# Turning the experts' rows on VectorE instead of TensorE, in an attention plus mixture-of-experts kernel

## The chip, the cores and the metric

The kernel runs on one core of a Trainium2 chip. A core has a matrix engine (TensorE, in the profile PE; PEld is its loading of the stationary operand), a vector engine (VectorE, DVE), an activation engine (ScalarE, ACT), a general one (GpSimd, POOL) and a sync engine (SP) that here only issues DMAs. Each engine works through its own queue in program order, and engines wait for one another by semaphores. The metric is the device time of one execution in microseconds (us), the median of several runs. Lower is better. The profile is of one execution, and its span is somewhat shorter than the timed runs.

## The reference, cut to what matters

Attention with a causal mask and a decay, then one expert of eight for each token. All data is float32.

```python
B, H, S, D = 8, 8, 576, 64             # attention
scores = q @ k.T / sqrt(D)
cum = cumsum(maximum(s, 0))
scores += minimum(-(cum[:, None] - cum[None, :]), 0)      # causal: later keys masked
x = softmax(scores) @ v                # heads side by side: (8, 576, 512)

E, F = 8, 1024                         # experts, rows of 512
logits = x @ w_gate
local_gate = sigmoid(x @ w_local)
for each batch b, position s:
    fresh_e = argmax(logits[b, s])
    e = fresh_e if s == 0 or local_gate[b, s] < 0.5 else prev_e
    prev_e = e
    h = maximum(x[b, s] @ w1[e], 0)    # 512 -> 1024, relu
    out[b, s] = softmax(logits[b, s])[e] * (h @ w2[e])    # 1024 -> 512, scaled by the gate
```

## The kernel before

The first part is attention, 32 pairs of heads, one step for each and one more. Beside it the tokens are sorted by expert: their rows are scattered to a buffer in DRAM (`rows_d`), each expert's rows one after another, with the token's number and its gate at the end of each row. The second part, `experts`, works through 26 units: two early ones of experts 0 and 1, and 24 that tables name at run time: "double" (256 rows of one expert), "single" (128 rows) and "mixed" (two halves of 64 rows of two experts). A block of 128 rows comes in with tokens on the partitions. The first layer needs it turned, features on the partitions, as `xT`. In the kernel before, TensorE turns a block by four transposes (128x128 each) into one PSUM bank, and VectorE copies the bank to `xT`. Then come the first layer into banks `hp` with a relu to `hT`, the second layer into a bank `yp`, the scaling of `yp` by the gate to `y`, and the scattering of `y`'s rows to the output.

The turning:

```python
    def __init__(self, nc, fx, gp, ident):
        self.nc, self.fx, self.gp, self.ident = nc, fx, gp, ident
        self.xT, self.at, self.gate = {}, {}, {}

    def product(self, i, k, n, x, ps):

        ps = self.ps = ps.rearrange("p (c n) -> p c n", c=DK)
        for c in range(DK):
            self.nc.tensor.transpose(ps[:, c, :], x[:, 2 * c * HW + X0 : 2 * c * HW + X0 + P], self.ident)
        if k == 0:
            self.xT[i] = self.fx.tile([P, DK * 2 * P], F32, name="xT")[:, : DK * n * P].rearrange(
                "p (c n) -> p c n", c=DK)

    def copies(self, i, k, x):

        nc = self.nc
        nc.vector.tensor_copy(self.xT[i][:, :, k * P : k * P + P], self.ps)
        both = self.gp.tile([P, 2], I32, name="at_gate")
        self.at[i, k], self.gate[i, k] = both[:, 0:1], both[:, 1:2].bitcast(F32)
        nc.vector.tensor_copy(self.at[i, k], x[:, XI : XI + 1])
        nc.vector.tensor_copy(self.gate[i, k], x[:, XI + 1 :])


```

In `experts` (the code for mixed units and the loads is cut):

```python
    ps_x = pool("ps_x", 1, space=PSUM)
    ps_h = pool("ps_h", 2, space=PSUM)
    ps_y = pool("ps_y", 2, space=PSUM)
    ps_r = pool("ps_r", 3, space=PSUM)
    # ... cut
    def turn_x(i, k):
        if i >= NU or k >= nbs[i]:
            return
        ps = ps_x.tile([P, DK * P], F32, name="xp")
        x = xg.pop((i, k))
        turned.product(i, k, nbs[i], x, ps)
        turned.copies(i, k, x)


    def layer1(i, first, last):
        # ... cut
        per = 512 // n
        for g in range(first, last, per):
            ps = ps_h.tile([P, 512], F32, name="hp")
            for j in range(per):
                f = (g + j) * P
                y = ps[:, j * n : j * n + n]
                if len(w) == 1:
                    for c in range(DK):
                        mm(y, lhsT=w[0][:, c, f : f + P], rhs=xT[i][:, c, :], start=(c == 0), stop=(c == DK - 1))
                # ... cut: mixed units, hooks
            to = hT[i][:, g : g + per]
            if g // per % 2:
                nc.vector.tensor_scalar_max(to, ps, 0.0)
            else:
                nc.scalar.activation(to, ps, Act.Relu)

    def layer2(i, k, then):
        ps = ps_y.tile([P, D], F32, name="yp")
        w = [ws[s][:, DK * F :].rearrange("p (c d) -> p c d", c=FK) for s in of[i]]
        m = P // len(w)
        for c in range(FK):
            for n, wn in enumerate(w):
                a = k * P + n * m
                mm(ps[n * m : n * m + m, :], lhsT=hT[i][:, c, a : a + m], rhs=wn[:, c, :],
                   start=(c == 0), stop=(c == FK - 1))
            if c in then:
                turn_x(*then[c])
            tick()
        y = gp.tile([P, D], F32, name="y", bufs=3)
        nc.vector.tensor_scalar_mul(y, ps, gate[i, k])
        nc.gpsimd.indirect_dma_start(
            out=next(outs)[:, :], out_offset=bass.IndirectOffsetOnAxis(ap=at[i, k][:, 0:1], axis=0),
            in_=y[:, :], element_offset=0, bounds_check=N - 1, oob_is_err=False, in_offset=None)

    def second(i):

        for k in range(nbs[i]):
            layer2(i, k, {3: (i + 2, k)} if nbs[i] == 2 else {1: (i + 2, 0), 5: (i + 2, 1)})
```

The order of the units; `load` requests weights, `fetch` requests rows, both ahead of their use:

```python
    layer1(0, 0, 4)
    turn_x(1, 0)
    layer1(0, 4, FK - 2 if nbs[0] == 2 else FK)
    turn_x(1, 1)
    if nbs[0] == 2:
        layer1(0, FK - 2, FK)
    if ready:

        layer1(1, 0, FK)
        load(0)
        fetch(2)
        fetch(3)
        for k in range(2):
            layer2(0, k, {})
        load(1)
        for k in range(2):
            layer2(1, k, {1: (2 + k, 0), 5: (2 + k, 1)})
        load(2)
        layer1(2, 0, 4)
        fetch(4)
        layer1(2, 4, FK)
    else:
        fetch(2)
    for i in range(2 if ready else 0, NU):
        load(i)
        layer1(i + 1, 0, 4)
        fetch(i + 3)
        layer1(i + 1, 4, FK)
        second(i)
```

The first unit's rows come in near the end of attention, and are turned in its steps 30 and 31:

```python
        at(27, 1, fetch_early)
        # ... cut
        for i in range(2):
            at(30 + i, 1, lambda bank, i=i: turned.product(0, i, 2, ready["x"][0, i], bank(1)[0]))
            at(30 + i, 2, lambda bank, i=i: turned.copies(0, i, ready["x"].pop((0, i))))
```

The last group of tokens (batches 6 and 7) is still sorted while the first expert units run: its instructions are hung between their matmuls (`tick`).

## Time and profile before

| | |
|---|---|
| time, median of 3 runs | 829.06 us (828.01 to 829.65) |
| span of the profiled execution | 815.2 us |
| attention, start to the first matmul of the experts | 0 to 248.1 us |
| last matmul ends, about | 808.3 us |
| mean granted clock of TensorE | 0.997 |

How to read the page: the first part gives each engine's busy time, share of the span and number of instructions. The second cuts the span in 40 slices and gives each engine's busy share in tenths. Groups of instructions are told by their line in the kernel, the engine, the operation, the tiles written and read, their shapes and number; behind the bar stand the busy time in us, the mean duration of one in ns, and how long the engine had idled before them and for whom. The groups that the change touches, beside the matmuls:

```profile
L1210 ACT ACTIVATE hT<-hp 128x512 f32<-128x512 f32 x38 | 22.7, 597 | 506.8 <-PE hp L1195 422.9
...
L1208 DVE TENSOR_SCALAR hT<-hp 128x512 f32<-128x512 f32 x38 | 26.2, 690 | 223.7 <-PE hp L1195 187.7
...
L1225 DVE TENSOR_SCALAR y<-yp,at_gate 128x512 f32<-128x512 f32 x38 | 28.5, 750 | 135.6 <-PE yp L1219 135.6
...
L1086 DVE COPY xT<-xp 128x512 f32<-128x512 f32 x36 | 24.9, 691 | 81.8 <-PE xp L1078 81.7
```

These are 38 relus on ScalarE and 38 on VectorE, 38 scalings of the output, and 36 copies of turned blocks (two more blocks, of the first unit, are turned in attention into a tile `bank`). A timeline lists instructions in order of time: start in us, duration of the run in us, engine, line, operation, tiles, shape, number, and in brackets the idle time before and its releaser. TensorE's matmuls in float32 show as two records each, its transposes as one.

### The profile page before, as it was taken

How to read it: one execution, taken by the hardware profiler on the slowest of the kernel's cores; microseconds unless marked ns; L12 is line 12 of the kernel's file. 1: busy time of each engine (PE TensorE's matmuls, PEld its weight loads, DVE VectorE, ACT ScalarE, POOL GpSimd, SP SyncE). 2: the span in 40 equal slices, each digit the busy share in tenths (PEclk: the TensorE clock that was granted, in tenths of full speed). 3: DMA queues.
4: the chain of work that ended last, by engine and by line, in shares of the span. 5: the costliest groups of instructions: out<-in, count | busy, mean ns of one | idle time of the engine just before them, and what ended most of it. 6: DMA issues, size and time to landing. Idle time of an engine off the chain costs nothing.

```text
span 815.2 us, 19716 instructions
## 1 busy us (share of the span) xinstructions
PE 798.7 (98%) x8118; PEld 595.9 (73%) x8118; DVE 213.9 (26%) x700; ACT 188.5 (23%) x535; POOL 176.4 (22%) x329
## 2 busy tenths in 40 slices
PE   9999999999999999999999899998999999999996
PEld 8989888888888748666776666775667766676762
DVE  2234434545535831111111111111111111111111
ACT  5767677576671000000000000000000000000000
POOL 4422344365350421001200011001111011011001
PEclk9999999999999999999999999999999999999999
DMA  9486589788735799678993779946599766994001
GB/s 323 146 293 199 165 266 328 267 275 254 230 135 208 213 402 393 252 249 292 358 388 142 248 254 362 389 174 248 161 358 391 273 200 203 358 411 151 21 15 42
DMA packets 64149, 204.57 MB, mean 251 GB/s; under 512 B 8269, under 2 KB 8301, under 8 KB 64048
## 3 DMA queue, kind: packets, MB, share of 16 engines
q1 hardware_dynamic: 55008, 172.41, 60.6%
q0 software_dynamic: 8896, 30.47, 9.9%
q8 instruction: 66, 1.08, 0.5%
q10 hardware_dynamic: 144, 0.33, 0.1%
q14 instruction: 35, 0.29, 0.1%
HBM read 179.93 MB, written 23.76 MB: 250 GB/s over the span
## 4 chain that ended last, share of the span: by engine, by line
PE 98%; issue 1%; POOL 0%; DVE 0%; POOLq 0%
PE yp L1219 32%; PE hp L1195 29%; PE o L407 13%; PE ps L329 11%; PE hp L1202 4%; PE o L369 2%; PE xp L1078 2%; PE o L285 1%; PE o L350 1%; PE bank L946 1%; PE bank L971 0%; PE bank L944 0%; PE bank L969 0%; PE bank L992 0%; PE bank L1078 0%
## 5 line engine op out<-in xcount | busy, mean ns | idle before, releaser
L1219 PE MATMUL yp<-w,hT 128*128 128x512 f32 (+1 forms) x528 | 221.1, 594 | 0.0
L1195 PE MATMUL hp<-xT,w 128*128 128x256 f32 (+1 forms) x1088 | 192.1, 337 | 0.0
L1195 PEld LDWEIGHTS hp<-xT,w 128*128 128x128 f32 x1088 | 172.1, 191 | 23.8 <-issue 7.8
L338 ACT ACTIVATE sc<-ps,bias 128x256 f32<-128x256 f32 (+3 forms) x448 | 156.5, 482 | 57.0 <-PE ps L329 55.0
L1219 PEld LDWEIGHTS yp<-w,hT 128*128 128x128 f32 (+1 forms) x528 | 88.0, 180 | 100.5 <-issue 99.5
L1210 ACT ACTIVATE hT<-hp 128x512 f32<-128x512 f32 x38 | 22.7, 597 | 506.8 <-PE hp L1195 422.9
L1226 POOL DMA_INDIRECT out_dram<-y,at_gate x38 | 38.5, 1012 | 461.7 <-DVE y L1225 446.8
L407 PEld LDWEIGHTS o<-v,sc 128*64 128x64 f32 x3072 | 108.8, 136 | 7.9 <-issue 5.2
L407 PE MATMUL o<-v,sc 128*64 128x74 f32 x3072 | 113.6, 229 | 0.1
L344 POOL TENSOR_SCALAR_AFFINE_SELECT sc<-sc 128x256 f32<-128x256 f32 x160 | 66.5, 420 | 122.0 <-issue 64.3
L329 PE MATMUL ps<-q,k 64*128 64x320 f32 (+2 forms) x768 | 92.2, 385 | 0.3 <-issue 0.3
L1208 DVE TENSOR_SCALAR hT<-hp 128x512 f32<-128x512 f32 x38 | 26.2, 690 | 223.7 <-PE hp L1195 187.7
L329 PEld LDWEIGHTS ps<-q,k 64*128 64x128 f32 x768 | 68.9, 186 | 15.1 <-ACT r_v L956 0.6
L1219 PE MATMUL yp<-x,hT 128*128 128x512 f32 (+1 forms) x144 | 65.6, 601 | 0.0
L1225 DVE TENSOR_SCALAR y<-yp,at_gate 128x512 f32<-128x512 f32 x38 | 28.5, 750 | 135.6 <-PE yp L1219 135.6
L1195 PEld LDWEIGHTS hp<-xT,x 128*128 128x128 f32 x320 | 46.1, 191 | 5.8 <-issue 2.6
L1195 PE MATMUL hp<-xT,x 128*128 128x128 f32 (+1 forms) x320 | 50.1, 317 | 0.0
L1086 DVE COPY xT<-xp 128x512 f32<-128x512 f32 x36 | 24.9, 691 | 81.8 <-PE xp L1078 81.7
L1037 POOL DMA_INDIRECT x_rows<-x,r_slot_i x40 | 38.7, 968 | 10.0 <-issue 5.9
L1219 PEld LDWEIGHTS yp<-x,hT 128*128 128x128 f32 (+1 forms) x144 | 25.0, 181 | 21.8 <-issue 21.4
L1202 PE MATMUL hp<-xT,w 128*64 128x64 f32 x768 | 32.5, 227 | 6.4 <-issue 6.4
L1202 PEld LDWEIGHTS hp<-xT,w 128*64 128x64 f32 x768 | 31.4, 141 | 9.9 <-issue 9.9
(164 smaller groups left out, 412.9 us busy)
## 6 DMA issues: line engine op xcount, KB each, us to landing
w<-in_w_dram SPq DMA_DIRECT2D x184, 512.0 KB, 10.1
x<-in_w_dram SPq DMA_DIRECT2D x56, 512.0 KB, 10.1
v<-in_vx_dram SPq DMA_DIRECT2D x32, 370.0 KB, 5.3
vt<-in_vz_dram SPq DMA_DIRECT2D x32, 320.0 KB, 4.1
k<-in_kz_dram SPq DMA_DIRECT2D x31, 320.0 KB, 5.3
q<-in_q_dram SPq DMA_DIRECT2D x32, 288.0 KB, 5.9
xg<-x_rows POOLq DMA_DIRECT2D x30, 293.0 KB, 8.3
x_rows<-r_empty SPq DMA_DIRECT2D x6, 293.0 KB, 5.0
```

The source lines that it names most:

```text
L329: mm(ps[:, h, at : at + z - a], lhsT=kb[d, c * P : c * P + P], rhs=qb[d, a:z], start=True, stop=True)
L338: nc.scalar.activation(scs[n, u][:, h, at : at + z - a], raw[u][:, h, at : at + z - a], Act.Exp, bias=bias[:, i : i + 1], scale=scale)
L344: nc.gpsimd.affine_select(out=x, in_=x, compare_op=Alu.is_ge, fill=0.0, base=0, pattern=[[0, 2], [1, P]], channel_multiplier=-1)
L407: mm(y, lhsT=w, rhs=x, start=start, stop=stop)
L1037: self.s.nc.gpsimd.indirect_dma_start(out=next(self.s.views)[:, :], out_offset=bass.IndirectOffsetOnAxis(ap=self.slot[:z, m : m + 1], axis=0),
L1086: nc.vector.tensor_copy(self.xT[i][:, :, k * P : k * P + P], self.ps)
L1195: mm(y, lhsT=w[0][:, c, f : f + P], rhs=xT[i][:, c, :], start=(c == 0), stop=(c == DK - 1))
L1202: mm(y[d, m], lhsT=w[h ^ swap][:, c, f + h * HALF : f + h * HALF + HALF], rhs=xT[i][:, c, m], start=(c == 0), stop=(c == DK - 1))
L1208: nc.vector.tensor_scalar_max(to, ps, 0.0)
L1219: mm(ps[n * m : n * m + m, :], lhsT=hT[i][:, c, a : a + m], rhs=wn[:, c, :], start=(c == 0), stop=(c == FK - 1))
L1225: nc.vector.tensor_scalar_mul(y, ps, gate[i, k])
L1226: nc.gpsimd.indirect_dma_start(out=next(outs)[:, :], out_offset=bass.IndirectOffsetOnAxis(ap=at[i, k][:, 0:1], axis=0), in_=y[:, :], eleme ...
```

## The change

Three things. VectorE turns the rows of all units but the second: one of its instructions turns 32 rows by 4 x 32 features, four squares of 32x32, and writes them to the 32 partitions of `xT` where they belong; 16 of them make a block, and no PSUM bank or copy is needed. They are issued a first layer ahead, before the first layer of the unit in between, instead of within the second layer of the unit two before. The first unit's rows are turned so in the last steps of attention, a quarter block or some at a time; the second unit's are still turned by TensorE. To make room on VectorE, the relus of the first layer and the scaling of the second layer's output all go to ScalarE. The PSUM bank that took the turned rows becomes a third one for the first layer.

```diff
--- before.py
+++ after.py
@@ -147,9 +147,10 @@
 
         fx = main.enter_context(tc.tile_pool(name="fx", bufs=2))
         turned = ready["turned"] = Turned(nc, fx, main.enter_context(tc.tile_pool(name="first", bufs=2)), ident)
-        for i in range(2):
-            at(30 + i, 1, lambda bank, i=i: turned.product(0, i, 2, ready["x"][0, i], bank(1)[0]))
-            at(30 + i, 2, lambda bank, i=i: turned.copies(0, i, ready["x"].pop((0, i))))
+        for j in range(8):
+            at((29, 29, 30, 30, 30, 31, 31, 31)[j], 2,
+               lambda bank, j=j: turned.squares(0, j // 4, 2, ready["x"][0, j // 4], (j % 4,)))
+        at(31, 2, lambda bank: [turned.extras(0, k, ready["x"].pop((0, k))) for k in range(2)])
         last = sort.group((6, 7), xs)
 
         attention(tc, q, kz, vz, vx, s, w_gate, w_local, ident, lg, recs, const, new_x, plan)
@@ -1071,19 +1072,33 @@
         self.nc, self.fx, self.gp, self.ident = nc, fx, gp, ident
         self.xT, self.at, self.gate = {}, {}, {}
 
+    def new(self, i, k, n):
+        if k == 0 and i not in self.xT:
+            self.xT[i] = self.fx.tile([P, DK * 2 * P], F32, name="xT")[:, : DK * n * P].rearrange(
+                "p (c n) -> p c n", c=DK)
+
+    def squares(self, i, k, n, x, quarters=range(4)):
+
+
+        self.new(i, k, n)
+        rows = x[:, :XI].rearrange("p (c w) -> p c w", w=2 * HW)
+        m = P // 4
+        for a in quarters:
+            for d in range(0, P, m):
+                self.nc.vector.transpose(self.xT[i][d : d + m, :, k * P + a * m : k * P + a * m + m],
+                                         rows[a * m : a * m + m, :, X0 + d : X0 + d + m])
+
     def product(self, i, k, n, x, ps):
 
-        ps = self.ps = ps.rearrange("p (c n) -> p c n", c=DK)
+        self.new(i, k, n)
+        ps = ps.rearrange("p (c n) -> p c n", c=DK)
         for c in range(DK):
             self.nc.tensor.transpose(ps[:, c, :], x[:, 2 * c * HW + X0 : 2 * c * HW + X0 + P], self.ident)
-        if k == 0:
-            self.xT[i] = self.fx.tile([P, DK * 2 * P], F32, name="xT")[:, : DK * n * P].rearrange(
-                "p (c n) -> p c n", c=DK)
-
-    def copies(self, i, k, x):
+        self.nc.vector.tensor_copy(self.xT[i][:, :, k * P : k * P + P], ps)
+
+    def extras(self, i, k, x):
 
         nc = self.nc
-        nc.vector.tensor_copy(self.xT[i][:, :, k * P : k * P + P], self.ps)
         both = self.gp.tile([P, 2], I32, name="at_gate")
         self.at[i, k], self.gate[i, k] = both[:, 0:1], both[:, 1:2].bitcast(F32)
         nc.vector.tensor_copy(self.at[i, k], x[:, XI : XI + 1])
@@ -1111,8 +1126,7 @@
     wp = pool("wp", 1)
     gp = pool("gp", 8)
     fp = pool("fp", 2)
-    ps_x = pool("ps_x", 1, space=PSUM)
-    ps_h = pool("ps_h", 2, space=PSUM)
+    ps_h = pool("ps_h", 3, space=PSUM)
     ps_y = pool("ps_y", 2, space=PSUM)
     ps_r = pool("ps_r", 3, space=PSUM)
     gx = gx or pool("gx", 5)
@@ -1168,13 +1182,15 @@
                     row = number(sort.rowi[kinds[kind]], j, ET.Pool, E * R)
                 nc.gpsimd.dma_start(x, rows_d[bass.ds(row + k * P, P), :])
 
-    def turn_x(i, k):
+    def turn_x(i, k, by_products=False):
         if i >= NU or k >= nbs[i]:
             return
-        ps = ps_x.tile([P, DK * P], F32, name="xp")
         x = xg.pop((i, k))
-        turned.product(i, k, nbs[i], x, ps)
-        turned.copies(i, k, x)
+        if by_products:
+            turned.product(i, k, nbs[i], x, bank(1)[0])
+        else:
+            turned.squares(i, k, nbs[i], x)
+        turned.extras(i, k, x)
 
     def layer1(i, first, last):
 
@@ -1203,13 +1219,10 @@
                                    rhs=xT[i][:, c, m], start=(c == 0), stop=(c == DK - 1))
                 for _ in range(nbs[i]):
                     tick()
-            to = hT[i][:, g : g + per]
-            if g // per % 2:
-                nc.vector.tensor_scalar_max(to, ps, 0.0)
-            else:
-                nc.scalar.activation(to, ps, Act.Relu)
-
-    def layer2(i, k, then):
+
+            nc.scalar.activation(hT[i][:, g : g + per], ps, Act.Relu)
+
+    def layer2(i, k):
         ps = ps_y.tile([P, D], F32, name="yp")
         w = [ws[s][:, DK * F :].rearrange("p (c d) -> p c d", c=FK) for s in of[i]]
         m = P // len(w)
@@ -1218,19 +1231,16 @@
                 a = k * P + n * m
                 mm(ps[n * m : n * m + m, :], lhsT=hT[i][:, c, a : a + m], rhs=wn[:, c, :],
                    start=(c == 0), stop=(c == FK - 1))
-            if c in then:
-                turn_x(*then[c])
             tick()
         y = gp.tile([P, D], F32, name="y", bufs=3)
-        nc.vector.tensor_scalar_mul(y, ps, gate[i, k])
+        nc.scalar.activation(y, ps, Act.Copy, scale=gate[i, k])
         nc.gpsimd.indirect_dma_start(
             out=next(outs)[:, :], out_offset=bass.IndirectOffsetOnAxis(ap=at[i, k][:, 0:1], axis=0),
             in_=y[:, :], element_offset=0, bounds_check=N - 1, oob_is_err=False, in_offset=None)
 
     def second(i):
-
         for k in range(nbs[i]):
-            layer2(i, k, {3: (i + 2, k)} if nbs[i] == 2 else {1: (i + 2, 0), 5: (i + 2, 1)})
+            layer2(i, k)
 
     if ready:
         ws[1] = room[1]
@@ -1240,34 +1250,40 @@
         fetch(0)
         fetch(1)
     if not ready:
-        for k in range(nbs[0]):
-            turn_x(0, k)
+        for i in range(2):
+            for k in range(2):
+                turn_x(i, k)
     tick(0)
     layer1(0, 0, 4)
-    turn_x(1, 0)
-    layer1(0, 4, FK - 2 if nbs[0] == 2 else FK)
-    turn_x(1, 1)
-    if nbs[0] == 2:
+    if ready:
+        turn_x(1, 0, True)
+        layer1(0, 4, FK - 2)
+        turn_x(1, 1, True)
         layer1(0, FK - 2, FK)
-    if ready:
 
         layer1(1, 0, FK)
         load(0)
         fetch(2)
         fetch(3)
         for k in range(2):
-            layer2(0, k, {})
+            layer2(0, k)
         load(1)
         for k in range(2):
-            layer2(1, k, {1: (2 + k, 0), 5: (2 + k, 1)})
+            turn_x(2, k)
+        second(1)
         load(2)
+        for k in range(2):
+            turn_x(3, k)
         layer1(2, 0, 4)
         fetch(4)
         layer1(2, 4, FK)
     else:
+        layer1(0, 4, FK)
         fetch(2)
     for i in range(2 if ready else 0, NU):
         load(i)
+        for k in range(2):
+            turn_x(i + 2, k)
         layer1(i + 1, 0, 4)
         fetch(i + 3)
         layer1(i + 1, 4, FK)
```

## The prediction

> **What bounds the kernel now.** I read the busy shares first, then the chain of waits, then the groups of instructions, and last the timelines around the instructions that the change touches.
>
> ```profile
> PE 798.7 (98%) x8118; PEld 595.9 (73%) x8118; DVE 213.9 (26%) x700; ACT 188.5 (23%) x535; POOL 176.4 (22%) x329
> ...
> PE 98%; issue 1%; POOL 0%; DVE 0%; POOLq 0%
> PE yp L1219 32%; PE hp L1195 29%; PE o L407 13%; PE ps L329 11%; PE hp L1202 4%; PE o L369 2%; PE xp L1078 2%; PE o L285 1%; PE o L350 1%; PE bank L946 1%; PE bank L971 0%; PE bank L944 0%; PE bank L969 0%; PE bank L992 0%; PE bank L1078 0%
> ```
>
> The matrix engine (PE) is busy for 98% of the 815.2 us span and is 98% of the chain that ended last. So the end moves by what leaves PE's own queue, or by new holes in it, and hardly by anything else. The turning of the experts' rows (xp, line 1078) is 2% of that chain: this is the whole prize. VectorE (DVE) and ScalarE (ACT) are about a quarter busy over all. By stages DVE is busy 38.7 us of the 92 us from 248 to 340 and 70.6 us of the 475 us after that; ACT 5.9 and 17.9 us.
>
> What a turned block of 128 rows costs PE is not its duration but the time to the next start. A typical one, in the timeline of PE:
>
> ```profile
> 401.43 0.60 PE L1078 MATMUL xp<-ident,xg 128*128 128x128 f32 x4
> 401.86 1.88 PE L1219 MATMUL yp<-w,hT 128*128 128x512 f32 x4
> ```
>
> From 401.43 to 401.86 is 0.43 us for four transposes, though each lasts 273 ns: they overlap. I went through all of PE's timeline from 250 to 790 us this way. Nearly every block costs 0.43 to 0.44 us, the four turned inside mixed units 0.58 or 0.59. In attention the two blocks of unit 0 take 0.59 us (236.55 to 237.14) and 0.73 us (243.95 to 244.68).
>
> On DVE, the end of attention:
>
> ```profile
> 244.28 0.19 DVE L374 COPY v<-o 128x45 f32<-128x45 f32 x1
> 244.39 0.19 DVE L375 COPY v<-o 128x45 f32<-128x45 f32 x1
> 244.64 0.69 DVE L1086 COPY xT<-bank 128x512 f32<-128x512 f32 x1
> 245.25 0.15 DVE L1089 CAST at_gate<-xg 128x1 int32<-128x1 f32 x1
> 245.31 0.15 DVE L1090 COPY at_gate<-xg 128x1 f32<-128x1 f32 x1
> 247.01 0.18 DVE L409 RECIPROCAL recs<-o 128x4 f32<-128x4 f32 x1 [1.56 <-PE o L407]
> ```
>
> The reader is to see the hole of 1.56 us before 247.01, the only room in this last step. The two small copies are 0.06 us apart though each lasts 0.15: DVE's instructions can overlap. PE starts the experts' first layer at 248.14.
>
> [...] 36 copies of 0.69 us follow the 144 transposes. [...] the trace has one table load (1.28 us) though exp and relu both run, [...] so a scaled copy should add none.
>
> **The change, part by part.** There are 38 blocks of 128 rows: 2 of unit 0 (in attention), 2 of unit 1, 34 of the others. Unit 1 stays on PE.
>
> (1) Taken from PE in the experts: 34 blocks, 30 at 0.437 us and 4 at 0.58: 13.1 + 2.3 = 15.4 us. (2) Taken from PE in attention: 0.59 + 0.73 = 1.3 us. Both lie on the chain, and together they are 16.7 us.
>
> (3) Added to DVE: 36 blocks of 16 transposes, each 32 partitions by 128 elements. Estimate of one from this trace: a copy of one element takes 144 ns, and copies of 45 and 512 elements take 195 and 691, a slope of 1.06 ns an element; so 144 + 127 x 1.06 = 279 ns. Held, 16 of them are 4.5 us a block and 161 us in all; overlapped as the small copies are, about 0.2 us apart, 3.2 us a block. Taken from DVE: 36 copies of 0.69 (24.9), 38 relus (26.2), 38 scalings (28.5), in all 79.6 us. DVE then stands near 295 us, a third of the span.
>
> (4) Added to ACT: 38 relus of 0.597 (22.7 us) and 38 scalings, which should be near that. A PSUM bank of the first layer takes PE 3.44 us to fill and ACT 0.6 to empty, and there are now three banks for it in place of two, so PE doesn't wait there.
>
> (5) Moved: a unit's rows are now turned during the first layer of the unit ahead of it, and needed after that unit's whole second layer. A double unit is 28 us of PE and 9 us of DVE, a single one 14 and 4.5. Its rows were requested one unit earlier still and land in about 8.3 us. The slot of xT that is overwritten belongs to a first layer that is already over. I see no wait for PE in the steady part. The tightest place is unit 2: its rows are requested at 287.1 to 288.3 and land near 295, DVE would turn them by about 304 to 305, and PE reaches them at 308.8 less what was saved until then (some 2 us): a slack of 2 us.
>
> (6) The end of attention. With the 0.59 us of the step before gone, DVE's last copy ends near 244.0. Then come 12 transposes: 3.4 us held, 2.4 overlapped, and four small copies. So xT is whole at about 247.4, while PE, 1.3 us early, asks for it at 246.8: a wait of 0.6 us, or none if they overlap. The last batch's reciprocals slip behind them too, but its routing on PE comes 5.2 us later and DVE has caught up by then.
>
> (7) The tail: the last scaling takes 0.75 us on DVE and some 0.6 on ACT: 0.15 gained.
>
> Sum: 15.4 + 1.3 - 0.6 + 0.15 = 16.2 us. 829.06 - 16.2 = 812.8; I round to 813.0, since small holes are likelier than small gifts.
>
> **The rivals.** (a) DVE becomes a wait: if one transpose took 0.5 us and not 0.28, a block would take 8 us, the wait at the end of attention 3 us, and unit 2 another 5; the gain would shrink to some 8 us, near 821. For it: no such instruction runs before, so its length is an estimate. Against it: in the steady part even this fits into the 14 us of a single unit.
>
> (b) Instruction supply. PE has unexplained holes in the mixed units' first layers:
>
> ```profile
> 356.37 3.01 PE L1202 MATMUL hp<-xT,w 128*64 128x64 f32 x94 [0.46 <-issue]
> ...
> 567.07 2.09 PE L1202 MATMUL hp<-xT,w 128*64 128x64 f32 x36 [3.38 <-issue]
> ```
>
> They add up to 6.4 us in four places, named issue and no engine, in stretches with many short instructions and busy DMA queues. A shift of 2% in time can make them larger or smaller; I allow 2 us either way, and the change touches neither cause.
>
> (c) The transfer of weights takes the place of PE: if the weights came no faster than they do now, an earlier PE would wait for them. Against it: the DMA share is 67% after 340 us and no wait of PE names a DMA; the sync queue itself waits 233 us for PE to release weight buffers. From 281 to 330 us the queues are full (over 400 GB/s), and there some of the gain might be lost for a while. That would make the gain some 14 us, or 815.
>
> (d) More than is counted: should the waits of (b) vanish, up to 6 us more, 807.
>
> **Range and chances.** Two per cent is 16.6 us, or 812.5, so the estimate sits almost on the line between two of the verdicts. The sum of what leaves PE is firm to half a microsecond; the wait at the end of attention is 0 to 1 us; the holes move it by 2 us. That gives 810.0 to 817.0 for 8 in 10, with more room above for (a) and (c). Faster by over 2%: 0.43. Within 2%: 0.54. Slower by over 2%: 0.03, since nothing that is added lies on PE.
>
> **What would show it.** PE's transposes should fall from 152 to 8, and PE's busy time by 16 to 17 us. The transposes on DVE should last near 0.28 us and follow each other at that distance. The first matmul of the experts should show a wait of about half a microsecond on DVE, and unit 2's first none. DVE should be near 295 us busy, ACT near 235. The prediction is wrong if PE's busy time falls as said and the span doesn't, which would be a new wait in front of a first layer, or if the transposes last far from 0.28 us, or if the holes of the mixed units change by more than 2 us.

## The result, and the profile after

The changed kernel takes 809.48 us (median; 807.45 to 810.63) against 828.53 us (827.79 to 829.65) for the kernel before in the same comparison. The ratio is 0.9766, with a 95% interval of 0.9742 to 0.9791: 19.05 us are gained. I had predicted 16.2 us and 813.0. The measured time lies half a microsecond under the range of 810 to 817.

The experiments ran on four chips: e1 to e4, e5 to e8, e9 to e11 and e12 to e15. The kernel before takes 827 to 829 us on three of them and 816 us on that of e9 to e11; its first profile, with a span of 815.2 us, looks like this last one. So I took a second profile of the kernel before, e1, whose span of 824.2 us is the one to hold against the 805.8 us of after.

The page after, first the busy shares, then three groups of instructions (busy time, mean ns of one, idle before):

```profile
PE 786.0 (98%) x7974; PEld 583.2 (72%) x7974; DVE 310.6 (39%) x1164; ACT 236.6 (29%) x611; POOL 174.5 (22%) x329
...
L1088 DVE STREAM_TRANSPOSE xT<-xg 32x128 f32<-32x128 f32 x576 | 174.1, 302 | 272.3 <-DMA xg<-x_rows 167.6
...
L1223 ACT ACTIVATE hT<-hp 128x512 f32<-128x512 f32 x76 | 45.1, 597 | 226.1 <-PE hp L1211 183.1
...
L1236 ACT ACTIVATE y<-yp,at_gate 128x512 f32<-128x512 f32 x38 | 26.1, 687 | 239.3 <-PE yp L1232 233.2
```

PE has 144 matmuls fewer, and is still 98% busy: it remains the bound. Its busy time is 18.2 us less than in e1 (804.2), where 16 to 17 were predicted. DVE has more work by nearly a half, and waits for rows 167.6 us, so it is far ahead of PE in the experts. All relus and scalings now stand in ACT's list.

The same place as in the prediction, a single unit's second layer. In the timeline of PE of e1, the kernel before:

```profile
405.19 1.88 PE L1219 MATMUL yp<-w,hT 128*128 128x512 f32 x4
406.91 0.60 PE L1078 MATMUL xp<-ident,xg 128*128 128x128 f32 x4
407.34 3.60 PE L1219 MATMUL yp<-w,hT 128*128 128x512 f32 x8
410.78 0.60 PE L1078 MATMUL xp<-ident,xg 128*128 128x128 f32 x4
411.22 1.88 PE L1219 MATMUL yp<-w,hT 128*128 128x512 f32 x4
412.94 1.24 PE L1195 MATMUL hp<-xT,w 128*128 128x256 f32 x5
```

In that of after:

```profile
403.37 7.03 PE L1232 MATMUL yp<-w,hT 128*128 128x512 f32 x16
410.24 2.11 PE L1211 MATMUL hp<-xT,w 128*128 128x256 f32 x9
```

From the first start to the next layer's: 7.75 us before, 6.87 after. Two blocks are gone, 0.44 us each, as predicted.

DVE at the end of attention, in the timeline of after, and PE at the experts' first matmul, in its own:

```profile
251.46 3.79 DVE L1088 STREAM_TRANSPOSE xT<-xg 32x128 f32<-32x128 f32 x12
```

```profile
255.39 5.42 PE L1211 MATMUL hp<-xT,w 128*128 128x256 f32 x24 [0.34 <-DVE xT L1088]
```

Twelve transposes in 3.79 us: one starts 0.32 us after the other and lasts 0.30. They don't overlap. PE waits 0.34 us for the last of them.

**Where the time went, by stages.** Each stage runs from its first matmul on PE to the next stage's first; the numbers (us) are worked out from PE's timelines, and the differences from the times before rounding. "Mixed" are the first layers of the four mixed units, "first two" those of units 0 and 1.

```
                              e1 (before)   after   difference
attention, to experts' start     254.6      255.4      +0.75
first two first layers            32.7       34.5      +1.7
mixed first layers, four          39.6       36.0      -3.55
all other first layers           210.6      210.6       0
all second layers                279.9      262.5     -17.3
after the last matmul              6.8        6.8       0
span                             824.2      805.8     -18.4
```

Of the 17.3 us of the second layers, 30 blocks at 0.44 are 13.2. The four blocks in mixed units are 0.73 each (the second layer goes from 7.75 to 7.02 us), 2.9 together. That is 16.1. The remaining 1.2 us are holes that sit in second layers. In e1, for example, the stage after the third mixed first layer takes 14.92 us, and the same stage after the other three 14.28.

So there are three places to explain: the mixed first layers gain 3.55 us that I had put down as zero, the first two first layers lose 1.7, and attention gains nothing. PE's waits show the first. Columns: total us, how often, the longest. The kernel before (e1):

```profile
PE hp L1202 <- issue: 6.1, 3, 3.0
...
PE hp L1195 <- DVE hT L1208: 1.0, 1, 1.0
```

After:

```profile
PE hp L1218 <- issue: 3.2, 4, 1.3
...
PE hp L1211 <- issue: 2.5, 3, 1.7
...
PE hp L1211 <- DVE xT L1088: 0.3, 1, 0.3
```

Line 1202 of before is line 1218 of after, the mixed units' matmuls. Their holes named "issue" fall from 6.1 to 3.2 us, and nothing of the change is meant for them. Lines 1195 and 1211 are the other units' matmuls. Before, PE waits 1.0 us there for a relu of DVE; after, it has three holes of 2.5 us in sum, which its timeline has between 286.3 and 289.6, in unit 1's first layer.

### The profile page after: what moved, and what is told of

Its sections match the earlier page's. It is cut to its first block, busy times and chain, and to the rows that moved or that the text cites. A ratio compares the mean times of both kernels' runs of the same rounds, so it can differ in the third digit from the quotient of the medians.

```text
span 805.8 us, 19973 instructions
## 1 busy us (share of the span) xinstructions
PE 786.0 (98%) x7974; PEld 583.2 (72%) x7974; DVE 310.6 (39%) x1164; ACT 236.6 (29%) x611; POOL 174.5 (22%) x329
## 4 chain that ended last, share of the span: by engine, by line
issue 58%; POOL 4%; POOLq 1%; DMA 0%; SPq 0%
POOL out_dram L1237 2%; POOL xg L1183 2%; POOLq L1158 1%; DMA x_rows<-r_empty 0%; SPq L808 0%; POOLq L1183 0%; POOLq L1237 0%; POOL xg L1179 0%; POOLq L1179 0%; POOLq L166 0%; SPq L804 0%
## 5 line engine op out<-in xcount | busy, mean ns | idle before, releaser
L1088 DVE STREAM_TRANSPOSE xT<-xg 32x128 f32<-32x128 f32 x576 | 174.1, 302 | 272.3 <-DMA xg<-x_rows 167.6
L1232 PE MATMUL yp<-w,hT 128*128 128x512 f32 (+1 forms) x528 | 216.4, 593 | 0.0
L1232 PEld LDWEIGHTS yp<-w,hT 128*128 128x128 f32 (+1 forms) x528 | 90.1, 180 | 113.1 <-issue 111.4
L408 PE MATMUL o<-v,sc 128*64 128x74 f32 x3072 | 118.3, 229 | 4.0 <-issue 3.1
L408 PEld LDWEIGHTS o<-v,sc 128*64 128x64 f32 x3072 | 111.2, 136 | 13.4 <-issue 9.8
L1223 ACT ACTIVATE hT<-hp 128x512 f32<-128x512 f32 x76 | 45.1, 597 | 226.1 <-PE hp L1211 183.1
L1236 ACT ACTIVATE y<-yp,at_gate 128x512 f32<-128x512 f32 x38 | 26.1, 687 | 239.3 <-PE yp L1232 233.2
L1232 PE MATMUL yp<-x,hT 128*128 128x512 f32 (+1 forms) x144 | 63.3, 594 | 0.0
L410 DVE RECIPROCAL recs<-o 128x4 f32<-128x4 f32 x64 | 12.1, 189 | 91.7 <-PE o L408 84.1
```

Of the source, the lines that this page charges most:

```text
L408: mm(y, lhsT=w, rhs=x, start=start, stop=stop)
L1088: self.nc.vector.transpose(self.xT[i][d : d + m, :, k * P + a * m : k * P + a * m + m], rows[a * m : a * m + m, :, X0 + d : X0 + d + m])
L1223: nc.scalar.activation(hT[i][:, g : g + per], ps, Act.Relu)
L1236: nc.scalar.activation(y, ps, Act.Copy, scale=gate[i, k])
```

## The experiments

The theories at the start. A: the gain is PE's own turning, 16 us, and a shift of the mixed units' holes, some 3 us; the work moved to ACT is worth nothing. B: freeing DVE from relus and scalings, with the third PSUM bank, is what brings the rest. C: the three microseconds above 16 are the chip's. For the last runs A was made sharper: the holes come from the supply of instructions, in pages of fixed size, so the number of instructions ahead of a mixed unit sets where in it the hole lies and how long it is.

**e1: the kernel before, unchanged.** No edit.

> The kernel before, unchanged, for a second profile. Theory A (the first profile's span of 815.2 us is an unusual execution, the usual one has more holes on PE during attention): the span lies near 826 us, the extra 10 us or so lie before the experts' first matmul, which then comes near 258 us and not 248, and the experts' part stays near 567 us. Rival B (the usual execution is slower in the experts' part, where the change then gains more than I counted): attention near 248 us, experts near 578.

Measured: ratio 1.0007 [0.9991, 1.0023], 827.58 us. The two profiles of before differ by 9 us in span, and their stages say where: attention 248.1 against 254.6, the first two first layers 31.4 against 32.7, the mixed ones 38.8 against 39.6. The second layers agree to half a microsecond (279.4 and 279.9). Of the 9 us, 6.5 lie in attention, so A of the expectation holds in the main. C falls for the second layers: the 17 us that the change takes out of them are there with either profile of before, and e5, on another chip than e1 to e4, has the 262.5 us of after again. Attention's time varies by 6.5 us between these two profiles of one kernel, and so a saving of one microsecond there can't be seen between two profiles.

**e2: the turning left out of the kernel before.** Of units 2 to 25 the rows are copied to `xT` unturned. It leaves the transposition out, so the output isn't the reference's; copies, relus and scaling stay as they were.

```diff
-        turned.product(i, k, nbs[i], x, ps)
+        if i < 2:
+            turned.product(i, k, nbs[i], x, ps)
+            turned.copies(i, k, x)
+            return
+        turned.ps = x[:, :XI].rearrange("p (c w) -> p c w", w=2 * HW)[:, :, X0 : X0 + P]
...
```

> The kernel before, but the 34 turned blocks of the later units leave out PE's transposes: VectorE copies the rows to xT unturned, so the output is not the reference's. Theory A (PE's transposes cost what the timeline showed, 0.43 to 0.58 us a block, and nothing more): 15.4 us less than before, ratio 0.981. Rival B (a turned block costs more in the usual execution, by what it does to PE's instruction supply or to waits): 18 us or more less, ratio 0.978 or below.

Measured: 0.9716 [0.9672, 0.9760], 804.73 us: 22.7 us less than the kernel before, so A of the expectation (15.4) falls and B (18 or more) holds. The second layers take 262.8 us, as after the change (262.5): the 17 us come from leaving out PE's transposes and from nothing else of the change. The mixed first layers take 34.5 us in place of 39.6, and the holes named "issue" shrink though nothing in those stages was edited. In the waits of PE of e2 line 1209 is the mixed units' matmul:

```profile
PE hp L1209 <- issue: 1.8, 4, 0.7
```

**e3: the first unit turned by PE.** The changed kernel, with unit 0 turned in attention as before.

```diff
-        for j in range(8):
-            at((29, 29, 30, 30, 30, 31, 31, 31)[j], 2,
-               lambda bank, j=j: turned.squares(0, j // 4, 2, ready["x"][0, j // 4], (j % 4,)))
...
+        for i in range(2):
+            at(30 + i, 1, lambda bank, i=i: turned.product(0, i, 2, ready["x"][0, i], bank(1)[0]))
...
```

> The changed kernel, but the first unit's rows are turned by TensorE in attention as before. Theory A (turning them on VectorE is worth 0.7 us, 1.3 saved and 0.6 lost in the wait at the first matmul): 0.7 us slower than the changed kernel, ratio to before 0.977 to 0.978. Rival B (the extra gain comes from attention): 3 us or more slower than the changed kernel, ratio 0.980 or above.

Measured: 0.9751 [0.9709, 0.9792], 807.14 us, not to be told from after. Attention takes 255.5 us (255.4 after). This part of the change, for which I had counted 0.7 us net, is worth nothing that these runs can see; a difference so small would be lost in what attention varies by. Beside it the mixed first layers take 33.7 us here, 2.3 less than after, and the second layers 264.1, 1.6 more, though only eight transposes in attention were put back.

**e4: only the work moved to ACT.** The kernel before, with all relus and the scaling of `y` on ACT.

```diff
-            to = hT[i][:, g : g + per]
-            if g // per % 2:
-                nc.vector.tensor_scalar_max(to, ps, 0.0)
-            else:
-                nc.scalar.activation(to, ps, Act.Relu)
+            nc.scalar.activation(hT[i][:, g : g + per], ps, Act.Relu)
...
-        nc.vector.tensor_scalar_mul(y, ps, gate[i, k])
+        nc.scalar.activation(y, ps, Act.Copy, scale=gate[i, k])
```

> The kernel before with only the relus and the scaling of the output moved to ScalarE; rows are turned by TensorE as before. Theory A (PE never waited for either): 0.15 us gained at the tail, ratio 0.999 to 1.001. Rival B (relus on VectorE held PE up somewhere in the usual execution): 2 to 3 us gained, ratio 0.997.

Measured: 1.0083 [1.0054, 1.0111], 833.98 us: this part alone makes the kernel before slower, and B falls as far as it does without a third bank (e8 has one). The waits of PE say by what:

```profile
PE hp L1195 <- ACT hT L1206: 6.6, 1, 6.6
PE hp L1202 <- issue: 5.2, 3, 3.3
```

One wait of 6.6 us for a relu, in the first layer of unit 1: the first two first layers take 41.1 us. ACT stands still there: it waits for nothing in the program that the trace shows. The same is seen after the change, in ACT's timeline:

```profile
276.64 0.60 ACT L1223 ACTIVATE hT<-hp 128x512 f32<-128x512 f32 x1 [2.86 <-PE hp L1211]
289.55 1.57 ACT L1223 ACTIVATE hT<-hp 128x512 f32<-128x512 f32 x3 [12.31 <-remote]
```

Three relus in a row at 289.55: the banks had long been full. ACT did nothing for 12.31 us, and the releaser that the trace gives, "remote", is no engine of this program. With three banks PE goes on filling banks for most of that time, with holes of 2.5 us in sum; with two it waits 6.6 us here. The holes of PE after the change that were left open above belong to this stand: the last of them ends at 289.56, when ACT starts again, and in e3, e5 and e12 too PE and ACT start again within 0.03 us of each other, though the trace calls PE's holes "issue"; in e9 and e10, where ACT doesn't stand, that layer has no holes. The kernel before has a wait of ACT of this length too (12.51 us in e1, where the trace names PE), but there DVE does every second relu, and PE loses 1.0 us by it.

**e5: the changed kernel again**, on the chip of the next three. No edit.

> The changed kernel, unchanged, as the measure of the other three on the same chip: ratio to before 0.974 to 0.979. In its profile the four first layers of the mixed units take 33.5 to 36.5 us together (39.6 in the kernel before), and the first two units' first layers about 34.5 (32.7 before).

Measured: 0.9779 [0.9754, 0.9804], 811.93 us. Attention takes 262.0 us here, the first two first layers 34.6 (ACT's stand is there again), the second layers 262.5, the mixed first layers 35.8.

**e6: two banks in place of three** in the changed kernel.

```diff
-    ps_h = pool("ps_h", 3, space=PSUM)
+    ps_h = pool("ps_h", 2, space=PSUM)
```

> The changed kernel with two PSUM banks for the first layer in place of three. Theory A (moving every relu to ScalarE costs some 6 to 7 us while ScalarE stands still in the second unit's first layer, and the third bank is what lets PE run past most of it): 4 to 6 us slower than the changed kernel, ratio to before 0.982 to 0.984, and the first two units' first layers take 39 to 41 us. Rival B (the third bank does nothing, PE is paced by its own instructions): no difference, 0.976.

Measured: 0.9818 [0.9790, 0.9846], 815.33 us; beside e5 3.4 us more, with intervals that just overlap. In the waits of PE:

```profile
PE hp L1211 <- ACT hT L1223: 6.7, 1, 6.7
```

The first two first layers take 40.9 us, 6.3 more than in e5, and the rest of the experts is as there to half a microsecond. The total differs by less than the expected 4 to 6 us. Attention, which the edit doesn't touch, takes 257.3 us in this profile and 262.0 in that of e5. So the third bank is needed only where ACT stands, in one stage, and there it hides some 6 us of it. In the rest of the experts two banks did as well.

**e7: every second relu of units 0 and 1 on DVE**, the rest as changed.

```diff
-            nc.scalar.activation(hT[i][:, g : g + per], ps, Act.Relu)
+            if ready and i < 2 and g // per % 2:
+                nc.vector.tensor_scalar_max(hT[i][:, g : g + per], ps, 0.0)
+            else:
+                nc.scalar.activation(hT[i][:, g : g + per], ps, Act.Relu)
```

> The changed kernel, but in the first two units every second relu is done by VectorE as before. Theory A (the 1.7 us that the first two units' first layers lost are ScalarE's stand): 1 to 2 us faster than the changed kernel, the first two first layers back at 32.5 to 33 us. Rival B (VectorE is late there too, with the routing of the last tokens): no gain, 34 us or more.

Measured: 0.9748 [0.9700, 0.9796], 809.23 us, 2.7 us under e5 with overlapping intervals. The first two first layers fall from 34.6 (e5) to 32.7 us, and the second layers of units 0 and 1 rise from 27.5 to 28.6: more than half is given back. Half of the relus avoid the ACT that stands; that the other half still wait for it is the likely reason, not a shown one.

**e8: squares only.** The changed kernel with relus alternating and the scaling on DVE, as before the change.

```diff
-            nc.scalar.activation(hT[i][:, g : g + per], ps, Act.Relu)
+            to = hT[i][:, g : g + per]
+            if g // per % 2:
+                nc.vector.tensor_scalar_max(to, ps, 0.0)
+            else:
+                nc.scalar.activation(to, ps, Act.Relu)
...
-        nc.scalar.activation(y, ps, Act.Copy, scale=gate[i, k])
+        nc.vector.tensor_scalar_mul(y, ps, gate[i, k])
```

> The changed kernel with relus and scaling where they were: every second relu and all scalings on VectorE, behind the squares. Theory A (VectorE is a third busy, a block's squares take 4.9 us against 14 us of a single unit, and three banks cover the delay): as fast as the changed kernel or up to 2 us faster. Rival B (VectorE's queue stands at a square that waits for its rows to land, up to 19 us, and the relus behind it hold PE up): 5 us or more slower than the changed kernel.

Measured: 0.9750 [0.9719, 0.9781], 809.20 us, 2.7 us under e5 with overlapping intervals. PE doesn't stall behind relus that queue up after waiting transposes on DVE: its waits of 0.5 us or more name no relu. That fear, the reason for moving them, isn't borne out with three banks. The first two first layers take 31.4 us against 34.6, and 1.3 us come back in the second layers after them.

**e9 and e10: a shift of PE's instructions.** The changed kernel with 48, or 32, products of one element ahead of the experts' first matmul. The profile counts two matmuls for each (8070 for e9, 7974 after), and as many loads: 192 or 128 instructions more. If pages of instructions make the holes, their places move.

```diff
     tick(0)
+    if ready:
+        some = bank(1)[0]
+        for _ in range(48):
+            mm(some[:1, :1], lhsT=ident[:1, :1], rhs=ident[:1, :1], start=True, stop=True)
     layer1(0, 0, 4)
```

> The changed kernel with 48 matmuls of 1x1 (192 instructions on PE) in front of the experts' first matmul; they compute nothing that is used and cost some 6 us themselves. Theory A (the holes in the mixed units' first layers are PE waiting for its next page [...], and their size depends on where the page's edge falls in the stage): the edge moves from about the 190th matmul of the stage to about the 222nd, where the kernel before had its 3 us hole, in all four mixed units alike; the four stages take 44 to 48 us together instead of 36. Rival B (the holes come from data, the stages take what they took): 34 to 37 us.

> The same with 32 such matmuls (128 instructions). Theory A: the edge falls at about the 126th and 254th matmul, where the kernel before had 2 us in its second mixed unit; the four stages take 38 to 41 us. Rival B: 34 to 37 us.

Measured, in one run each, on the chip where the kernel before takes 816.31: 812.13 us with 48, 803.93 with 32; since the kernel before varies from 810.7 to 819.0 there, these two times say little. The mixed first layers take 42.6 us in e9 and 40.2 in e10, and in both 3.2 us of holes more lie in the second layers after them. After the change they take 36.0, but on another chip: the changed kernel itself wasn't run on this one. The expectation of e10 (38 to 41) was met, that of e9 (44 to 48) only if the holes in second layers are counted. So the sizes are weak evidence. In the waits of PE of e9, line 1218 against 3.2 us in after:

```profile
PE hp L1218 <- issue: 9.3, 4, 2.8
```

The place tells it best. A mixed first layer has 256 matmuls. The first of the four in PE's timeline of after, of e9 and of e10:

```profile
359.00 6.11 PE L1218 MATMUL hp<-xT,w 128*64 128x64 f32 x191
366.01 2.09 PE L1218 MATMUL hp<-xT,w 128*64 128x64 f32 x65 [0.90 <-issue]
```

```profile
354.02 6.75 PE L1218 MATMUL hp<-xT,w 128*64 128x64 f32 x223
362.91 1.20 PE L1218 MATMUL hp<-xT,w 128*64 128x64 f32 x33 [2.13 <-issue]
```

```profile
348.17 7.68 PE L1218 MATMUL hp<-xT,w 128*64 128x64 f32 x255
357.68 0.27 PE L1218 MATMUL hp<-xT,w 128*64 128x64 f32 x1 [1.83 <-issue]
```

The hole of the four units lies after matmul 191, 186, 182 and 177 in after; after 223, 218, 213 and 209 in e9; after 255, 250, 245 and 241 in e10. Between e9 and e10 the edit is 16 products, 32 matmuls in the records, and each of the four holes lies 32 matmuls later. Counted from the first matmul of the whole kernel, the four holes lie after 5541, 6176, 6811 and 7447 matmuls in e9 and, to the matmul, in e10, and after 5413, 6048, 6684 and 7319 in after: 127 or 128 earlier, which with their loads are 254 to 256 instructions. So the hole keeps its place in the queue of instructions, not in time and not in the unit's work, and the places that these runs show lie 127 or 128 matmuls apart. In what follows a page is this stretch, and its edge the place where a hole can lie.

**e11: PE transposes put back.** The changed kernel with 136 transposes of a constant at the old places, into a bank that nobody reads.

```diff
+            if ready and c in then and then[c][0] < NU and then[c][1] < nbs[then[c][0]]:
+                some = bank(1)[0]
+                for j in range(DK):
+                    tr(some[:, j * P : j * P + P], ident, ident)
...
```

> The changed kernel with the 136 transposes of the later units put back on PE where they were, of a constant, into a bank that nobody reads: PE's queue is as before, while the rows are still turned by VectorE. Theory A (all of the gain is PE's queue: 17.3 us of the transposes and their surroundings, 3 to 4 us of the page's edges): 19 to 22 us slower than the changed kernel, ratio to before 1.000 to 1.005, mixed first layers back at 38.5 to 40 us. Rival B (part of the gain is that PE's transposes waited for rows or for the bank): only 15.4 us slower, ratio 0.995, mixed first layers at 36.

Measured: 0.9972 [0.9952, 0.9992], 813.33 us against 816.31. The second layers are back at 279.8 us, those of the kernel before (279.4 and 279.9): 17.3 us, on a kernel that has all else of the change. Of these 16.1 are the transposes, stage by stage as in the difference of e1 and after, and 1.2 a hole in the stage after the third mixed first layer. The mixed first layers take 36.5 us, where I expected them near before's 39; the ratio, expected at 1.000 or above, is a little below. Eight transposes of unit 0 are still missing from PE's queue, so the count ahead of the mixed units isn't that of the kernel before. That fits A, but I had not foreseen it.

**e12: the changed kernel a third time.** No edit; it stands beside the next three, on their chip.

> The changed kernel, unchanged, as the measure of the other three on this chip: ratio to before 0.974 to 0.979, the four first layers of the mixed units 35 to 37 us together with the page's edge at about the 190th matmul.

Measured: 0.9756 [0.9721, 0.9791], 808.18 us. The mixed first layers take 35.7 us.

**e13: the holes moved out.** In the changed kernel ten of the idle products at the very start are replaced by 30 of one element, 40 matmuls more in all (8014 for 7974), so that the edge of a page should fall 40 matmuls earlier in the mixed first layers, after 151 to 137 in place of 191 to 177.

```diff
-    spin(18)
+    spin(8)
+    for i in range(30):
+        mm(banks[1][:1, :1], lhsT=ident[:1, :1], rhs=ident[:1, :1], start=True, stop=True)
```

> The changed kernel with 10 of the 18 idle matmuls that PE runs at the very start replaced by 30 of 1x1, which take the same 3.5 us but are 80 instructions more. Nothing else changes. Theory A (the place of the page's edge sets the holes): the edge moves from about the 190th to about the 140th to 155th matmul of each mixed first layer, where the earlier runs had holes of 0 to 0.5 us, so the four stages take 31 to 34 us and the kernel is 2 to 4 us faster than the changed one. Rival B (the place hardly matters, the holes only follow how full the DMA queues are): 35 to 37 us, no difference in time.

Measured: 0.9731 [0.9695, 0.9767], 806.21 us. The four mixed first layers take 7.98, 7.99, 7.96 and 7.97 us, 31.9 in all; that is a mixed first layer without a hole. The first two of them, 512 matmuls, in the view of one line of e13 (count, ns, first and last start, then what its engine waited for ahead of it):

```profile
L1220 PE MATMUL hp<-xT,w x384: 217/222/271, 363.5 to 469.9; 128*64 128x64 f32 x192
L1220 PE MATMUL hp<-xT,x x128: 222/222/270, 462.1 to 469.8; 128*64 128x64 f32 x128
its engine sat idle before it (us, times) until:
```

The list under "sat idle" is empty: in these 512 matmuls no wait of PE of 0.15 us or more is seen. By the count of matmuls the edge of a page still falls inside these layers, only earlier. The profiles of all runs agree on this: a hole after 209 or more matmuls of such a layer is 1.4 to 3.4 us long, where the edge by this count falls after 162 to 201 there are 0 to 2.3 us, and in the eight mixed layers of e13 and e15, with the edge after 137 to 151, one hole of 0.7 us.

The total gains 2.0 us beside e12 (the intervals overlap), and the profiles' spans differ by 0.9 (806.2 and 807.1), less than the 3.8 us that left these stages: a hole came up in the second layers of units 0 and 1 (28.8 us for 27.5), and attention took 1.3 us more.

**e14 and e15: the best combination.** e14 is the kernel of e8 again. e15 is that kernel with e13's edit at the start.

> Squares on VectorE, with relus and scaling left where they were before, once more. Theory A (moving relus and scaling to ScalarE is worth nothing and costs 1 to 2 us where ScalarE stands still): 1 to 2 us faster than the changed kernel. Rival B (the last time's lead was chance): equal within 1 us.

> Both together: squares only, and the page's edge moved by 80 instructions. Theory A: 3 to 6 us faster than the changed kernel, ratio to before 0.970 to 0.973. Rival B: like the squares alone.

Measured: e14 0.9725 [0.9687, 0.9763], 806.15 us, with the first two first layers at 31.4 us and the mixed ones at 36.2; e15 0.9700 [0.9663, 0.9737], 804.01 us. In e15 the mixed first layers take 32.8 us and the first two 32.9. It is 4.2 us under the changed kernel on the same chip (e12); its interval overlaps that of e12 at the edge and lies clear of that of the result (0.9742 to 0.9791).

## Why the prediction was right, and where it failed

By the terms of its sum, in us gained:

```
term                              predicted   measured
(1) blocks in the experts           15.4        16.1
(b) holes in the mixed units         0 +-2       4.8   (3.55 there, 1.2 in second layers)
(4) work moved to ACT                0          -1.7
(2)+(6) first unit, less the wait    0.7         none seen
(7) tail                             0.15        0
```

For the pair of profiles e1 and after: 16.1 + 4.8 - 1.7 = 19.2, less the 0.75 that attention took longer, is 18.4, the difference of the spans.

**The step that failed** is the end of rival (b): "I allow 2 us either way, and the change touches neither cause." It touches what these holes hang on. The change takes 136 transposes and their loads, 272 instructions, out of PE's queue in the experts, and the holes keep to places in that queue. e9 and e10 showed that the count of instructions alone, with little work, moves them within their units (32 matmuls fewer ahead, and each lies 32 matmuls later); e13, beside e12 on one chip, showed that it can take them out (31.9 us for 35.7). e2 showed it on the kernel before: without the transposes, and with nothing of the squares, the mixed first layers drop by 5 us. What I called a rival with "up to 6 us more, 807", was the course it took, in part. The prediction's own sign of being wrong came with it: the holes of the mixed units changed by more than 2 us, from 6.1 to 3.2. That it was a gain, and of this size, is luck of where the edges fell: with the same turning on DVE these stages take 31.9 us in e13 and, on another chip, 42.6 in e9.

What ties it to pages is the DMA view. The page of before has this line among its queues (packets, MB, share):

```profile
q8 instruction: 66, 1.08, 0.5%
```

These are packets of 16 KB, for a PE that shows 8118 matmuls and as many loads, 246 to a packet; the holes of e9 and after lie 127 or 128 matmuls apart, with their loads 254 to 256. So the distance of the places is near the count for one packet. The holes in these stages are up to 3.4 us long. PE around the third mixed unit of e1, in its timeline:

```profile
566.61 7.00 PE L1202 MATMUL hp<-xT,w 128*64 128x64 f32 x220
576.57 2.19 PE L1202 MATMUL hp<-xT,w 128*64 128x64 f32 x36 [2.96 <-issue]
```

The queues of the half microsecond from 574.0 to 574.5 in e1 (packets, MB, share of the 16 engines); in the half microsecond ahead of it the last line is missing:

```profile
q1 hardware_dynamic: 30, 0.11, 55.9%
q0 software_dynamic: 29, 0.09, 43.0%
q8 instruction: 1, 0.02, 11.7%
```

PE runs dry at 573.6, one packet of instructions moves beside queues of weights (q1) and rows (q0) that take 99% of the DMA engines' time between them, and PE starts again at 576.57. In the mixed units of all runs such a hole ends 2.2 to 3.6 us after the start of such a packet (2.3 to 2.5 in before, 2.2 to 3.0 in after). And of the stages of the experts only these pass so many instructions so quickly: 256 matmuls, with their loads about two packets by that count, in 7.97 us (e13), while a second layer's 16 take 6.87. That PE waits there for the packet is my reading of this order in time. What isn't shown is why it would come late: whether it is asked for too late or waits behind the weights. The weights' queue has 76 to 83% of the DMA engines' time in all four mixed first layers of e1, the most in the one that has no hole, and no run here took the transfers away and left the rest.

**Term (4), ACT.** "PE doesn't wait there" holds in the steady part, by e6 even with two banks, and the third bank is why it nearly holds for units 0 and 1 (2.5 us of holes in after, a wait of 6.7 us with two banks in e6). There ACT is idle for 12.3 us on three of the four chips, where its usual wait for a bank is 2.86, and the first two first layers take 1.7 us longer. The relus that DVE did before were a way round it, and the change took that away. e4, e8 and e14 agree that the move to ACT brings nothing: with three banks it costs 3 us in these two layers (34.6 in e5, 31.4 in e8), of which 1.3 came back behind them, and with two banks 8.4 (41.1 in e4, 32.7 in e1). The first profile of before couldn't show the stand, because it isn't in it: there, as in e10 and e11, these two layers take 31.4 us. The scaled copies brought no new table load: ACT has one of 1.28 us in before and one in after.

No run tried what ACT waits for. The traces give a hint. SP issues eight transfers that clear rows at that time, in after:

```profile
274.62 15.35 SPq L808 DMA_DIRECT2D x_rows<-r_empty  x8
```

and in e9, where ACT doesn't stand:

```profile
272.71 9.91 SPq L808 DMA_DIRECT2D x_rows<-r_empty  x8
```

In all profiles with the stand these eight issues take 14.0 to 15.5 us, and ACT starts again within half a microsecond of their end; in those without it they take 9.8 to 11.7. So two engines are held until nearly the same moment, which may have one cause outside both of them; nothing shows which.

**Term (1)** was right in kind and 0.7 us too small. For the four mixed blocks I had taken the 0.58 us between the transposes' start and the next start, and left out a gap of 0.15 us ahead of them. e11 put the same instructions back and found 16.1 us, beside a hole of 1.2.

**Term (3), DVE.** I estimated 279 ns for one transpose from two copies; it is 302, and they start 0.315 us apart (16 in 5.04 us). Of the prediction's two cases, 4.5 us a block held and 3.2 overlapped, it is the first: none of the 576 in after starts before the one ahead of it has ended. What keeps them apart isn't shown. DVE is busy 310.6 us, not 295, and rival (a) falls as argued: DVE waits for rows (167.6 us), and PE waits for DVE's turning once, 0.34 us.

**Terms (2), (6) and (7).** The wait at the experts' start was predicted at 0.6 us and is 0.34. Still, no run shows a gain of the first unit: e3, without it, takes the same time. Nor could it be seen: attention takes 257.3 to 262.0 us in the profiles of e5 to e8, on one chip and with the same attention. Tail: 0.15 us predicted, nothing to be seen.

**Point (5)** held: unit 2's first layer takes 27.85 us in both kernels, with no wait for its rows. Rival (c) stayed out as well: no wait of PE names a transfer of weights.

## What to carry to other kernels

If one engine is 98% busy and sets the end, count what leaves its queue by the distance of starts, not by durations, and take the gap ahead of a group with it: that gave 16 of the 19 us to within a microsecond here. But if the profile shows holes named "issue" in stretches of very short instructions, removing or adding instructions earlier in that engine's queue can move them, as in e9 and e10 (by 32 matmuls); find their place in counts of instructions, see how late in the stretch it lies, and give the range room for all of them. Work moved to an engine with "room on average" should be looked at in the one stage where that engine stands (here ACT, 29% busy after the change, for 12.3 us).

## What the runs showed of the hardware that I had not expected

- The place of an instruction in PE's queue has a cost of its own: 40 matmuls more at the very start, the one edit to the changed kernel in e13, bring the mixed first layers from 35.7 to 31.9 us on one chip. The holes are 0.2 to 3.4 us each, at places in the queue of instructions that lie 127 or 128 matmuls with their loads apart (e9 and e10 against after).
- ACT is idle for 12.3 to 12.7 us in one stage on three chips of four, in the kernel before and in all versions of the changed one, and not on the fourth. Eight of SP's issues take longer at the same time, 14.0 to 15.5 us where ACT stands and 9.8 to 11.7 where it doesn't.
- Chips differ more than most changes: the same kernel before takes 816 us on one chip and 827 to 829 us on three; between the two profiles of it 6.5 of 9 us are in attention. What is compared has to run on one chip, and even there attention varied by 4.7 us between profiles (e5 and e6).
